# A fused attention, gated-MLP and normalised-MLP kernel on one core: first-block subtractions, weight loads, and places of tiles in SBUF

## The chip, the cores and the metric

One core of a Trainium2 chip (trn2) runs the whole kernel in one launch. The metric is device time in microseconds (us) of that core, median of several runs; lower is better. Engines are called as in the profile: PE (TensorE matmuls), PEld (TensorE weight loads), DVE (VectorE), ACT (ScalarE), POOL (GpSimd), SP (SyncE, which issues all DMAs here). TensorE's clock has two levels, 1.2 and 2.4 GHz; the profile shows which was granted.

## What is computed

Three stages, each fed by the one before; all in float32.

```python
# attention, chunked: 8 batches x 8 heads x 9 chunks of 64 positions, head size 64
attn = softmax(q_c @ k_c.T / 8);  x = attn @ v_c            # -> 4608 tokens x 512
# gated MLP, 512 -> 2048 -> 512
h = x @ w_in;  g = h * clip(h + 3, 0, 6) / 6;  x = g @ w_out
# second MLP, 512 -> 1024 -> 512
h = x @ w_in2; s = h * softmax(h); ln = (s - mean(s)) / sqrt(var(s) + 1e-6) * g_ln
out = ln @ w_out2
```

## The kernel before

**Split products.** Each large matrix product is made of three matmuls in the type float32r: every operand is held as a high part (a rounding cast on ACT, `split`, L73) and a low part (source minus high part, a subtraction on DVE or POOL, L74), and hi x hi, lo x hi and hi x lo are added up in PSUM. One such matmul is 128x128 (stationary, a weight load of its own each time) by 128x512 (moving). There are 5184 of them: 9 blocks x 16 slices x 24 in the gated MLP and 36 tiles x 48 in the second MLP.

**Weights.** The weights arrive as 64-bit words that hold doubles (`fetch`, L127). Each 128x512 slice is turned into a float32 pair in steps: `rescale` (L139, ACT, one operation), `convert` (L144, DVE: one `bitwise_and` for the sign, L152, and two shift-and-or operations, L157), then `split_w` (L170: the cast on ACT, the subtraction on POOL). `wi` are slices of w_in, `wo` of w_out.

**Order.** The program is in a hand-written order; each engine takes its own instructions strictly in the order in which the code issues them. First comes a start section (L322 to L377): four attention units (128 tokens each, scores, softmax, transposition, product with v) that make block 0's input. Then the gated MLP runs over 9 blocks of 512 tokens (L428 to L458). A block has 16 slices f: `moe_h` (L267, 12 matmuls into `hp`, then a Relu on ACT), `moe_g` (L281: the gate on DVE, L282, then the split of g into `g_hi`, `g_lo`), and, one slice later, `moe_o` (L292, 12 matmuls into four `acc` tiles). `slot` puts the attention work of the next block between them, one unit per four slices. In block 0 the weights are still being converted: each slice also issues `convert(("o", f), ("i", f + 3))`, and the subtractions for `g_lo`, `wo` and `wi` are on POOL. The result of a block goes to DRAM (`x2d`). In the second MLP a tile of 128 tokens takes 24 matmuls in `h2` (L474, stationary x, moving `wi`) and 24 in `out_t` (L557, stationary `l_hi` and `l_lo`, moving `wi`), with the softmax and normalisation on ACT, DVE and POOL between them.

**Loads at the start.** SP issues in order: q and k of four units, v, and among them w_in slices 0, 1, w_out slice 0, w_in 2, w_out 1, the norm weights; then q and k of unit 4, v of units 4 and 5, q and k of unit 5 (L367), and only then the remaining weights (L368 to L374).

**Places in SBUF.** The pools are laid out one after the other, and each tile is rounded up to 32 bytes per partition. The first large tile starts at byte 17088 of a partition (16384 reserved, four constants of 32, `ident` 512, `three` 32, `g_sb` 32), which is 64 past a multiple of 128; everything large behind it has a size that is a multiple of 2048, so x, `wi`, `wo`, `g_hi` and `g_lo` all start 64 bytes past a multiple of 128. In the second MLP, pool `b2` has small tiles (128x1 numbers, 32 bytes each, two buffers) between the large ones; behind them `l_hi` and `l_lo` (pool `b3`) come to stand exactly on a multiple of 128 (173056 and on). All offsets inside these tiles that a matmul uses are multiples of 512 bytes.

Of the kernel before, what the change touches and what calls it, by code (L numbers as in the profile page):

```python
# [8 lines left out]
F32 = mybir.dt.float32  # L9
F32R = mybir.dt.float32r  # L10
# [6 lines left out]
P = 128  # L17
# [4 lines left out]
def tile_kernel(  # L22
# [120 lines left out]

    def convert(*keys):  # L144

        work = []
# [4 lines left out]
        for key, r, s in work:  # L151
            nc.vector.tensor_single_scalar(  # L152
                out=s, in_=r[:, :, 1], scalar=-(1 << 31), op=ALU.bitwise_and
            )
        for w, op, shift in ((0, ALU.logical_shift_right, 29), (1, ALU.logical_shift_left, 3)):
            for key, r, s in work:
                nc.vector.scalar_tensor_tensor(  # L157
                    out=s, in0=r[:, :, w], scalar=shift, in1=s, op0=op, op1=ALU.bitwise_or
                )
        for (kind, f), r, s in work:  # L160
            w = s.bitcast(F32)
            if kind == "2" and f >= KD * NS:
                nc.vector.tensor_scalar_mul(
                    out=w, in0=w, scalar1=g_sb[:, f - KD * NS : f - KD * NS + 1]
                )
            t = SLOTS[kind](f, F32R)
# [41 lines left out]

    def attn_exp_act(u):
        sc, mx = exps.pop(u)  # L210
        p_t[u] = att_tile(ap2, "p")
        sums[u] = ap2.tile([P, H], F32, tag="sm", name="sm")
        for h in range(H):
# [41 lines left out]

    def attn_pv(u, pb, x_hi, x_lo, ps=att_psum):
# [8 lines left out]
        split(x_hi[:, :, o : o + P], x_lo[:, :, o : o + P], xps)  # L265

# [13 lines left out]

    def moe_g(hp, t, eng):  # L281
        nc.vector.scalar_tensor_tensor(  # L282
            out=t, in0=t, scalar=6.0, in1=hp, op0=ALU.min, op1=ALU.mult
        )
        g_hi = gp.tile([P, BT], F32R, tag="g_hi", name="g_hi")
        g_lo = gp.tile([P, BT], F32R, tag="g_lo", name="g_lo")
        split(g_hi, g_lo, t, eng)
        return g_hi, g_lo
# [31 lines left out]
    vs = wo_slot(NF - 7, F32).rearrange("p c (h k) -> p c h k", h=H)  # L320

    load_qk(0)  # L322
    load_qk(1, qps[0][:, 0], diagonal(kbs[1], nc.gpsimd))
    load_qk(2, qps[1][:, 0], diagonal(kbs[2], nc.vector))
    fetch("i", 0)
    load_qk(3, qps[2][:, 0], diagonal(kbs[3], nc.gpsimd))
    load_v(0)
    load_v(1)
    fetch("i", 1)
    load_v(2, vs[:, 0])  # L330
    load_v(3, vs[:, 1])
    fetch("o", 0)
    fetch("i", 2)
    fetch("o", 1)
    nc.sync.dma_start(out=g_sb, in_=g_ln)
    make_identity(nc, ident)
    diagonal(pbd, nc.gpsimd)
    nc.gpsimd.memset(three, 3.0)
    xs = new_x()
    attn_scores(0)  # L340
    attn_scores(1)
    load_qk(4)
    attn_norm(0, nc.gpsimd)
# [3 lines left out]
    attn_norm(1)
    attn_scores(3, h_psum, qps[1][:, 1])
    attn_transpose(1, kbs[1])
    attn_norm(2)  # L350
    attn_pv(0, pbd, *xs)
# [14 lines left out]
    attn_scores_act(4)
    load_qk(5)  # L367
    for f in range(2, NF):  # L368
        if f < NF - 7:
            fetch("o", f)  # L370
        if f + 1 < NF:
            fetch("i", f + 1)
    for f in range(NF - 7, NF):
        fetch("o", f)  # L374
    convert(("i", 2))
    rescale("o", 0)
    rescale("i", 3)  # L377
# [25 lines left out]
    def slot(b, f):  # L403
        ph = (f + 1) % 4
        u = (b + 1) * UPB + (f + 1) // 4
        if ph == 0:
            w = u - 1
            if w < NU:
                attn_pv(w, pbd, *xn[w // UPB])
                p_t.pop(w, None)  # L410
                load_v(w + 2)
            start_scores(u)
        elif u < NU:
            first = u < 2 * UPB
            if ph == 1:
                if u in exps:
                    attn_exp_act(u)
                attn_norm(u)
            elif ph == 2 and not first:
                attn_transpose_dve(u, (0, 1))  # L420
# [53 lines left out]
    def h2(t):  # L474
# [19 lines left out]
        mu = b2.tile([P, 1], F32, tag="mu", name="mu")  # L494
        nc.vector.scalar_tensor_tensor(
# [150 lines left out]
```

## Time and profile before

| | us |
|---|---|
| median of 3 runs | 1312.58 (1311.85 to 1313.03) |
| the profiled execution | 1311.98 |
| its span in the trace | 1310.0 |
| start section, to the first `hp` matmul of block 0 | 27.81 |
| block 0, from there to the first matmul of block 1 | 119.02 |
| block 1 (blocks 2 to 6 are as long) | 95.93 |
| PE busy | 1277.4 (98%) |
| DVE, ACT, POOL busy | 794.0, 581.8, 298.5 |

How to read it: the profiled execution lies 0.6 us under the median, and 2 us of it lie outside the span. A "busy" PE counts a matmul from its start to its end; since successive matmuls overlap, that says little on how fast they follow each other. For this the starts of a group and of the next one are used: the difference, divided by the number of matmuls, is called the spacing here.

### The profile page before, as it was taken

What the parts mean: (1) busy time and instruction counts of PE and PEld (TensorE: products, weight loads), DVE (VectorE), ACT (ScalarE), POOL (GpSimd) and SP (SyncE); (2) the same over time, 40 slices, a digit from 0 to 9 for tenths busy, and PEclk for the clock granted to TensorE, in tenths of its full rate; (3) what the DMA queues carried; (4) which work ended last, traced back from release to release, by engine and by line L of the source; (5) the groups of instructions that cost most, each with busy time, mean ns of one, the idle gap of its engine ahead of it and who ended that gap; (6) DMA issues with size and microseconds to landing.
All of it is one profiled execution on the core that took longest, in us unless ns stands there. A gap on an engine that the chain in (4) does not pass through costs nothing.

```text
span 1310.0 us, 17877 instructions
## 1 busy us (share of the span) xinstructions
PE 1277.4 (98%) x6368; PEld 1041.7 (80%) x6368; DVE 794.0 (61%) x1556; ACT 581.8 (44%) x1106; POOL 298.5 (23%) x562
## 2 busy tenths in 40 slices
PE   6699999999999999999999999999999999999998
PEld 5566788888888888888888888888888888888887
DVE  6788655655655655656555555469766555555542
ACT  4566422222322222222322222445687666666665
POOL 2465200000000000000000000355355444444444
PEclk9899999999999999999999999999999999999999
DMA  7910110110110210200200200444132221222111
GB/s 236 409 62 25 57 49 25 57 49 25 58 47 25 77 29 25 81 25 25 81 25 28 78 25 1 129 129 129 28 94 82 80 81 49 81 81 73 57 49 57
DMA packets 52649, 92.41 MB, mean 71 GB/s; under 512 B 9552, under 2 KB 18768, under 8 KB 52560
## 3 DMA queue, kind: packets, MB, share of 16 engines
q1 hardware_dynamic: 52560, 91.27, 21.8%
q8 instruction: 50, 0.82, 0.2%
q14 instruction: 39, 0.32, 0.1%
HBM read 62.92 MB, written 18.87 MB: 62 GB/s over the span
## 4 chain that ended last, share of the span: by engine, by line
PE 89%; issue 3%; POOL 3%; DVE 2%; DMA 1%; ACT 1%; SPq 1%; POOLq 0%; ACTq 0%; DVEq 0%
PE acc L298 27%; PE hp L272 26%; PE po L564 15%; PE hp L482 15%; PE att L261 2%; PE att L186 2%; POOL g_lo L74 1%; POOL wo L74 1%; DMA wi<-in_moe_w_in 1%; DVE s L157 1%; POOL wi L74 1%; DVE s L152 1%; SPq L112 0%; DVE x_lo L74 0%; DVE t L282 0%
## 5 line engine op out<-in xcount | busy, mean ns | idle before, releaser
L298 PE MATMUL acc<-g_hi,wo 128*128 128x512 f32 x1152 | 295.0, 397 | 16.1 <-ACT wo L73 14.2
L272 PE MATMUL hp<-x_hi,wi 128*128 128x512 f32 x1152 | 285.1, 390 | 0.0
L298 PEld LDWEIGHTS acc<-g_hi,wo 128*128 128x128 f32 x1152 | 213.1, 189 | 73.1 <-ACT wo L73 18.9
L278 ACT ACTIVATE t<-hp,three 128x512 f32<-128x512 f32 x144 | 99.0, 687 | 372.6 <-PE hp L272 372.2
L272 PEld LDWEIGHTS hp<-x_hi,wi 128*128 128x128 f32 x1152 | 215.9, 188 | 44.9 <-ACT wi L142 0.2
L282 DVE SCALAR_TENSOR_TENSOR t<-t,hp 128x512 f32<-128x512 f32 x144 | 99.1, 688 | 234.4 <-ACT t L278 234.4
L74 POOL TENSOR_TENSOR g_lo<-t,g_hi 128x512 fp32r<-128x512 f32 x32 | 45.8, 1431 | 715.1 <-PE acc L298 672.5
L482 PE MATMUL hp<-wi,x_hi 128*128 128x512 f32 x576 | 177.8, 390 | 0.0
L298 PE MATMUL acc<-g_lo,wo 128*128 128x512 f32 x576 | 154.4, 390 | 0.0
L272 PE MATMUL hp<-x_lo,wi 128*128 128x512 f32 x576 | 153.9, 389 | 0.0
L564 PE MATMUL po<-wi,l_hi 128*128 128x512 f32 x576 | 140.2, 396 | 0.0
L251 DVE STREAM_TRANSPOSE pbd<-p 32x128 f32<-32x128 f32 x448 | 135.3, 302 | 5.7
L73 ACT CAST g_hi<-t 128x512 fp32r<-128x512 f32 x144 | 89.3, 620 | 107.9 <-DVE t L282 107.9
L564 PEld LDWEIGHTS po<-wi,l_hi 128*128 128x128 f32 x576 | 108.3, 188 | 25.6
L482 PEld LDWEIGHTS hp<-wi,x_hi 128*128 128x128 f32 x576 | 108.2, 188 | 23.5
L298 PEld LDWEIGHTS acc<-g_lo,wo 128*128 128x128 f32 x576 | 108.6, 189 | 22.9
L74 POOL TENSOR_TENSOR l_lo<-m,l_hi 128x1024 fp32r<-128x1024 f32 x36 | 86.6, 2406 | 174.1 <-ACT l_hi L73 152.0
L272 PEld LDWEIGHTS hp<-x_lo,wi 128*128 128x128 f32 x576 | 108.1, 188 | 22.5
L74 DVE TENSOR_TENSOR g_lo<-t,g_hi 128x512 fp32r<-128x512 f32 x112 | 77.6, 693 | 76.8 <-ACT g_hi L73 76.8
L516 ACT COPY m<-tr 32x256 f32<-32x256 f32 x288 | 115.8, 402 | 2.9
L482 PE MATMUL hp<-wi,x_lo 128*128 128x512 f32 x288 | 112.4, 390 | 0.0
L491 ACT ACTIVATE e<-hp,nmx 128x1024 f32<-128x1024 f32 x36 | 40.2, 1116 | 111.3 <-DVE nmx L488 111.3
(91 smaller groups left out, 1299.7 us busy)
## 6 DMA issues: line engine op xcount, KB each, us to landing
wi<-in_moe_w_in SPq DMA_DIRECT2D x24, 512.0 KB, 7.3
x2d<-xo SPq DMA_DIRECT2D x36, 256.0 KB, 2.8
xo<-x2d SPq DMA_DIRECT2D x36, 256.0 KB, 4.3
m<-tr SPq DMA_DIRECT2D x288, 32.0 KB, 1.8
out<-ob SPq DMA_DIRECT2D x36, 256.0 KB, 2.2
v<-in_v SPq DMA_DIRECT2D x34, 256.0 KB, 2.6
q<-in_q SPq DMA_DIRECT2D x33, 256.0 KB, 3.5
kbd<-in_k SPq DMA_DIRECT2D x66, 128.0 KB, 3.5
```

Source lines behind the costliest of these rows:

```text
L73: nc.scalar.copy(out=hi, in_=src)
L74: (eng or nc.vector).tensor_sub(out=lo, in0=src, in1=hi.bitcast(F32))
L186: nc.tensor.matmul(sc[r0 : r0 + D, h // 2], qt[:, h], kt[:, :, h], start=True, stop=True)
L251: nc.vector.transpose(out=pb[o : o + 32, s // 2, c, s % 2], in_=pv[s * 32 : s * 32 + 32, c, e],)
L272: nc.tensor.matmul(hp, wi[f][:, a, kk * P : (kk + 1) * P], b[:, kk], start=(n == 0), stop=(n == 3 * KD - 1),)
L278: nc.scalar.activation(out=t, in_=hp, func=AF.Relu, bias=three[:])
L282: nc.vector.scalar_tensor_tensor(out=t, in0=t, scalar=6.0, in1=hp, op0=ALU.min, op1=ALU.mult)
L298: nc.tensor.matmul(acc[dc], wo[f][:, w, dc * P : (dc + 1) * P], g[i], start=(f == 0 and n == 0), stop=(f == NF - 1 and n == 2),)
L482: nc.tensor.matmul(hp[:, s * DM : (s + 1) * DM], a[:, kk, o : o + P], wi[kk * NS + s][:, w], start=(n == 0), stop=(n == 3 * KD - 1),)
L491: nc.scalar.activation(out=e, in_=hp, func=AF.Exp, bias=nmx, accum_out=r)
L516: move(out=m[b * 32 : b * 32 + 32, a], in_=tr[a * 32 : a * 32 + 32, b])
L564: nc.tensor.matmul(po, a[:, f], wi[KD * NS + f][:, w], start=(n == 0), stop=(n == 3 * NF2 - 1),)
```

## The change

1. **Subtractions.** In block 0 the subtractions for `g_lo`, `wo` and `wi` move from POOL to DVE; one softmax normalisation of the start (unit 2) moves from DVE to POOL. Conversion and split are cut into smaller functions so that they can be interleaved: in each slice of block 0 DVE now takes the gate, a first weight subtraction, the next signs, `g_lo`, the other weight subtractions, and then the shift-and-or operations. A w_out slice is converted one slice earlier than before. In the start section the scores go to the idle `acc` PSUM tiles and the first products with v to `hp` tiles.
2. **Weights queued first.** Two weight loads follow the loads of unit 4's q and k, others follow v of units 4 and 5; q and k of unit 5 and the norm weights come later.
3. **Projection operands at equal places.** The small tiles of the second MLP get a pool of their own (`bs`) behind the large ones, and `l_hi`, `l_lo` become six named single tiles. With that (and 4.) they stand at the same place modulo 2048 as x, `wi`, `wo`, `g_hi` and `g_lo`.
4. **64 bytes.** `three` is allocated with 17 columns instead of 1 (68 bytes, rounded to 96), so every large tile behind it moves by 64: the first starts at 17152, a multiple of 128, and so do all the others, `l_hi` and `l_lo` included.

The number and shapes of the matmuls are unchanged. The core of the diff:

```diff
-    three = const.tile([P, 1], F32, name="three")
+    three = const.tile([P, 17], F32, name="three")[:, :1]
...
+    def split_w_hi(n=1):
+        while ready and n:
+            hi, lo, w = ready.pop(0)
+            nc.scalar.copy(out=hi, in_=w)
+            halves.append((hi, lo, w))
+            n -= 1
+
+    def split_w_lo(eng):
+        for hi, lo, w in halves:
+            eng.tensor_sub(out=lo, in0=w, in1=hi.bitcast(F32))
+        halves.clear()
...
-    attn_scores(2, h_psum, qps[0][:, 1])
-    attn_transpose(0, pbd, h_psum)
-    rescale("i", 0)
+    attn_scores(2, acc_psum(2), qps[0][:, 1])
+    attn_transpose(0, pbd)
...
+    split_w(1, nc.vector)
     rescale("i", 1)
-    attn_transpose(3, kbs[3], h_psum)
-    split_w(1)
-    attn_pv(2, kbs[2], *xs)
+    attn_pv(2, kbs[2], *xs, h_psum, lo=False)
+    rescale("o", 0)
...
     pend = []
+    ahead = [[("o", f + 1), ("i", f + 3)] for f in range(NF)]
+    ahead[0].insert(0, ("i", 2))
...
-            h = moe_h(f, *xn[b])
+            hp, t = moe_h(f, *xn[b])
+            moe_gate(hp, t)
             if first:
-                split_w(1)
-            pend.append((b, f, moe_g(*h, nc.gpsimd if first or last else nc.vector)))
+                split_w(1, nc.vector)
+                g = moe_split(t, nc.vector, lambda: convert_signs(*ahead[f]))
+                split_w_hi(4)
+                split_w_lo(nc.vector)
+                convert_words()
+            else:
+                g = moe_split(t, nc.gpsimd if last else nc.vector)
+            pend.append((b, f, g))
             if f % 4 == 3:
                 slot(b, f)
-            if first:
-                convert(("o", f), ("i", f + 3))
...
-    b3 = ctx.enter_context(tc.tile_pool(name="b3", bufs=3, reuse_waits="tile"))
+    b3 = ctx.enter_context(tc.tile_pool(name="b3", bufs=1, reuse_waits="tile"))
+    bs = ctx.enter_context(tc.tile_pool(name="bs", bufs=2, reuse_waits="tile"))
...
-        l_hi = b3.tile([P, NF2, P], F32R, tag="l_hi", name="l_hi")
-        l_lo = b3.tile([P, NF2, P], F32R, tag="l_lo", name="l_lo")
+        l_hi, l_lo = l_tile("l_hi", t % 3), l_tile("l_lo", t % 3)
```

How it moves instructions, at the three places that the prediction speaks of. First SP, the DMA queue, from the first weights on. Before:

```order
L135 DMA wo_133<-in_moe_w_out 128x1024
L135 DMA wi_135<-in_moe_w_in 128x1024
L135 DMA wo_137<-in_moe_w_out 128x1024
L335 DMA g_sb<-in_moe_g_ln 128x8
L110 DMA q<-in_q 128x512
L112 DMA kbd<-in_k 64x512 x2
L120 DMA v<-in_v 128x512 x2
L110 DMA q<-in_q 128x512
L112 DMA kbd<-in_k 64x512 x2
L135 DMA wo_336<-in_moe_w_out 128x1024
L135 DMA wi_338<-in_moe_w_in 128x1024
```

Now:

```order
L135 DMA wo_133<-in_moe_w_out 128x1024
L135 DMA wi_135<-in_moe_w_in 128x1024
L110 DMA q<-in_q 128x512
L112 DMA kbd<-in_k 64x512 x2
L135 DMA wo_178<-in_moe_w_out 128x1024
L135 DMA wi_180<-in_moe_w_in 128x1024
L120 DMA v<-in_v 128x512
L135 DMA wo_250<-in_moe_w_out 128x1024
L135 DMA wi_252<-in_moe_w_in 128x1024
L120 DMA v<-in_v 128x512
L135 DMA wo_283<-in_moe_w_out 128x1024
L135 DMA wi_285<-in_moe_w_in 128x1024
```

The fourth w_in slice (`wi_338` before, `wi_180` now) moved from behind the second q and k pair to right behind the first.

Second, DVE from the scores of unit 4 (`mx<-att`) to the gate of slice 0 (`t<-t,hp`). Before:

```order
L205 TENSOR_REDUCE mx<-att 128x8
L206 TENSOR_SCALAR mx<-mx 128x8
L152 TENSOR_SCALAR s<-wi_135 128x512
L157 SCALAR_TENSOR_TENSOR s<-wi_135,s 128x512 x2
L282 SCALAR_TENSOR_TENSOR t<-t,hp 128x512
```

Now, to the first `g_lo`:

```order
L223 TENSOR_REDUCE mx<-att 128x8
L224 TENSOR_SCALAR mx<-mx 128x8
L151 TENSOR_SCALAR s<-wi_131 128x512
L159 SCALAR_TENSOR_TENSOR s<-wi_131,s 128x512 x2
L151 TENSOR_SCALAR s<-wo_133 128x512
L186 TENSOR_TENSOR wi_387<-s,wi_387 128x512
L159 SCALAR_TENSOR_TENSOR s<-wo_133,s 128x512 x2
L311 SCALAR_TENSOR_TENSOR t<-t,hp 128x512
L186 TENSOR_TENSOR wo_394<-s,wo_394 128x512
L151 TENSOR_SCALAR s<-wi_135 128x512
L151 TENSOR_SCALAR s<-wo_178 128x512
L321 TENSOR_TENSOR g_lo<-t,g_hi 128x512
```

The second w_in slice and the first w_out slice are now converted between the scores and the first gate, and three subtractions stand on DVE.

Third, one later slice of block 0 on DVE. Before:

```order
L282 SCALAR_TENSOR_TENSOR t<-t,hp 128x512
L152 TENSOR_SCALAR s<-wo_336 128x512
L152 TENSOR_SCALAR s<-wi_346 128x512
L157 SCALAR_TENSOR_TENSOR s<-wo_336,s 128x512
L157 SCALAR_TENSOR_TENSOR s<-wi_346,s 128x512
```

Now:

```order
L311 SCALAR_TENSOR_TENSOR t<-t,hp 128x512
L186 TENSOR_TENSOR wo_479<-s,wo_479 128x512
L151 TENSOR_SCALAR s<-wo_283 128x512
L151 TENSOR_SCALAR s<-wi_285 128x512
L321 TENSOR_TENSOR g_lo<-t,g_hi 128x512
L186 TENSOR_TENSOR wi_480<-s,wi_480 128x512
L159 SCALAR_TENSOR_TENSOR s<-wo_283,s 128x512
L159 SCALAR_TENSOR_TENSOR s<-wi_285,s 128x512
```

In both, two more shift-and-or operations follow. A slice has seven DVE operations before and ten now; POOL has three subtractions per slice before and none now. The weights subtracted now (`wo_479`, `wi_480`) were shifted one slice earlier.

## Rows read from the trace of the kernel before

**Rows 1.** The page: busy times; the chain that ended last, by engine.

```profile
PE 1277.4 (98%) x6368; PEld 1041.7 (80%) x6368; DVE 794.0 (61%) x1556; ACT 581.8 (44%) x1106; POOL 298.5 (23%) x562
PE 89%; issue 3%; POOL 3%; DVE 2%; DMA 1%; ACT 1%; SPq 1%; POOLq 0%; ACTq 0%; DVEq 0%
```

**Rows 2.** Busy time by stretch: window, length, engines with counts, clock, DMA.

```profile
27.81:47.98 20.17, 10.59 (x39) 8.31 (x38) 15.34 (x21) 10.56 (x30) 8.52 (x6) 0.75 0.92 354
47.98:146.83 98.85, 92.35 (x482) 69.67 (x481) 80.10 (x113) 59.31 (x137) 53.93 (x40) 1.00 0.30 108
146.83:242.76 95.93, 95.93 (x514) 79.07 (x513) 57.04 (x127) 28.75 (x58) 1.29 (x1) 1.00 0.15 45
935.00:1283.50 348.50, 348.50 (x1513) 284.06 (x1512) 198.07 (x389) 243.33 (x486) 163.34 (x424) 1.00 0.23 70
```

**Rows 3.** The chain in order of time, second MLP: start, length, what.

```profile
907.82 21.76 PE hp L482 x96
...
1195.18 5.60 PE po L564 x24
1200.78 5.47 PE hp L482 x24
...
1283.71 22.41 PE po L564 x96
```

**Rows 4.** PE's timeline in block 6: start, length, matmuls; one slice from start to start.

```profile
703.95 1.98 PE L272 MATMUL hp<-x_hi,wi 128*128 128x512 f32 x8
...
709.39 0.39 PE L272 MATMUL hp<-x_hi,wi 128*128 128x512 f32 x1
```

**Rows 5.** PE's timeline: matmuls at 1.2 GHz; transpositions at 2.4 GHz, four and one.

```profile
43.12 3.78 PE L298 MATMUL acc<-g_hi,wo 128*128 128x512 f32 x8 [9.58 <-ACT wo L73]
...
43.71 2.77 PE L298 MATMUL acc<-g_hi,wo 128*128 128x512 f32 x6
...
46.70 1.43 PE L298 MATMUL acc<-g_lo,wo 128*128 128x512 f32 x4
...
138.81 0.60 PE L236 MATMUL att<-ident,p 128*128 128x128 f32 x4
...
138.81 0.27 PE L236 MATMUL att<-ident,p 128*128 128x128 f32 x1
```

**Rows 6.** PE's timeline where `h2` follows `out_t`.

```profile
1200.61 0.62 PE L482 MATMUL hp<-wi,x_hi 128*128 128x512 f32 x2
...
1202.00 0.62 PE L482 MATMUL hp<-wi,x_hi 128*128 128x512 f32 x2
```

**Rows 7.** Timeline of the first slices of block 0.

```profile
35.80 0.65 ACT L142 ACTIVATE wi<-wi 128x512 f32<-128x512 f32 x1 [5.99 <-DMA wi<-in_moe_w_in]
36.35 0.67 ACT L278 ACTIVATE t<-hp,three 128x512 f32<-128x512 f32 x1
...
43.12 0.80 PE L298 MATMUL acc<-g_hi,wo 128*128 128x512 f32 x1 [9.58 <-ACT wo L73]
```

**Rows 8.** Timeline in block 0: DVE alone, then DVE beside POOL.

```profile
62.10 0.42 DVE L152 TENSOR_SCALAR s<-wi 128x512 int32<-128x512 int32 x1
62.44 0.69 DVE L157 SCALAR_TENSOR_TENSOR s<-wo,s 128x512 int32<-128x512 int32 x1
63.04 0.69 DVE L157 SCALAR_TENSOR_TENSOR s<-wi,s 128x512 int32<-128x512 int32 x1
...
66.36 1.29 POOL L74 TENSOR_TENSOR wi<-s,wi 128x512 fp32r<-128x512 f32 x1
66.40 1.54 DVE L152 TENSOR_SCALAR s<-wo 128x512 int32<-128x512 int32 x1
```

**Rows 9.** Groups of instructions: count, busy, mean ns of one, idle before.

```profile
L282 DVE SCALAR_TENSOR_TENSOR t<-t,hp 128x512 f32<-128x512 f32 x144 | 99.1, 688 | 234.4 <-ACT t L278 234.4
L74 DVE TENSOR_TENSOR g_lo<-t,g_hi 128x512 fp32r<-128x512 f32 x112 | 77.6, 693 | 76.8 <-ACT g_hi L73 76.8
L228 DVE TENSOR_TENSOR p<-p,sm 128x512 f32<-128x512 f32 x33 | 26.8, 811 | 1.1
```

More of the change, by code (lines that the diff above doesn't have):

```diff
@@ L142, in rescale, with convert_signs @@
             nc.scalar.activation(out=r, in_=r, func=AF.Copy, scale=2.0**-112)
-    def convert(*keys):
-        work = []
+    work, ready, halves = [], [], []
+    def convert_signs(*keys):
         for key in keys:
@@ L150, in convert, with convert_words @@
                 work.append((key, raws.pop(key).bitcast(I32), s))
[L151 to L154, printed above, removed]
+                nc.vector.tensor_single_scalar(
+                    out=s, in_=work[-1][1][:, :, 1], scalar=-(1 << 31), op=ALU.bitwise_and
+                )
+    def convert_words():
         for w, op, shift in ((0, ALU.logical_shift_right, 29), (1, ALU.logical_shift_left, 3)):
@@ L168, in convert, with split_w @@
             ready.append((t[:, 0], t[:, 1], w))
-    def split_w(n=2):
+        work.clear()
+    def convert(*keys):
+        convert_signs(*keys)
+        convert_words()
+    def split_w_hi(n=1):
         while ready and n:
-            split(*ready.pop(0), nc.gpsimd)
+            hi, lo, w = ready.pop(0)
+            nc.scalar.copy(out=hi, in_=w)
+            halves.append((hi, lo, w))
             n -= 1
+    def split_w_lo(eng):
+        for hi, lo, w in halves:
+            eng.tensor_sub(out=lo, in0=w, in1=hi.bitcast(F32))
+        halves.clear()
+    def split_w(n=2, eng=None):
+        split_w_hi(n)
+        split_w_lo(eng or nc.gpsimd)
     def att_psum():
@@ L207, in attn_scores_act, with attn_exp_act @@
         exps[u] = sc, mx
[L209 to L213, printed above, removed]
+    def attn_exp_act(u, heads):
+        sc, mx = exps[u]
+        if u not in sums:
+            p_t[u] = att_tile(ap2, "p")
+            sums[u] = ap2.tile([P, H], F32, tag="sm", name="sm")
+        for h in heads:
             nc.scalar.activation(
@@ L254, in attn_transpose_dve, with attn_pv @@
                     )
-    def attn_pv(u, pb, x_hi, x_lo, ps=att_psum):
+    def attn_pv(u, pb, x_hi, x_lo, ps=att_psum, lo=True):
         vt = v_t.pop(u)
@@ L264, in attn_pv, with attn_lo @@
         o = (u % UPB) * P
-        split(x_hi[:, :, o : o + P], x_lo[:, :, o : o + P], xps)
+        hi, lo_ = x_hi[:, :, o : o + P], x_lo[:, :, o : o + P]
+        nc.scalar.copy(out=hi, in_=xps)
+        los.append((lo_, xps, hi))
+        if lo:
+            attn_lo()
+    los = []
+    def attn_lo():
+        lo, xps, hi = los.pop(0)
+        nc.vector.tensor_sub(out=lo, in0=xps, in1=hi.bitcast(F32))
     def moe_h(f, x_hi, x_lo):
@@ L279, in moe_h, with moe_gate @@
         return hp, t
-    def moe_g(hp, t, eng):
+    def moe_gate(hp, t):
         nc.vector.scalar_tensor_tensor(
@@ L284, in moe_g, with moe_split @@
         )
+    def moe_split(t, eng, between=None):
         g_hi = gp.tile([P, BT], F32R, tag="g_hi", name="g_hi")
         g_lo = gp.tile([P, BT], F32R, tag="g_lo", name="g_lo")
-        split(g_hi, g_lo, t, eng)
+        nc.scalar.copy(out=g_hi, in_=t)
+        if between:
+            between()
+        eng.tensor_sub(out=g_lo, in0=t, in1=g_hi.bitcast(F32))
         return g_hi, g_lo
@@ L320, in tile_kernel, with acc_psum, later @@
     vs = wo_slot(NF - 7, F32).rearrange("p c (h k) -> p c h k", h=H)
+    def acc_psum(i):
+        return lambda: ps_acc.tile([P, DM], F32, tag=f"acc{i}", name=f"acc{i}")
+    def later(f):
+        if f < NF:
+            fetch("i", f)
     load_qk(0)
@@ L328, in tile_kernel @@
     load_v(1)
-    fetch("i", 1)
+    fetch("i", 0)
     load_v(2, vs[:, 0])
     load_v(3, vs[:, 1])
+    fetch("i", 1)
     fetch("o", 0)
     fetch("i", 2)
-    fetch("o", 1)
-    nc.sync.dma_start(out=g_sb, in_=g_ln)
     make_identity(nc, ident)
@@ L339, in tile_kernel @@
     xs = new_x()
-    attn_scores(0)
-    attn_scores(1)
+    attn_scores(0, acc_psum(0))
+    attn_scores(1, acc_psum(1))
     load_qk(4)
+    fetch("o", 1)
+    fetch("i", 3)
     attn_norm(0, nc.gpsimd)
-    attn_scores(2, h_psum, qps[0][:, 1])
-    attn_transpose(0, pbd, h_psum)
-    rescale("i", 0)
[L347 to L351, printed above, removed]
+    attn_scores(2, acc_psum(2), qps[0][:, 1])
+    attn_transpose(0, pbd)
+    attn_norm(1)
+    attn_scores(3, acc_psum(3), qps[1][:, 1])
+    attn_transpose(1, kbs[1])
+    rescale("i", 0)
+    attn_norm(2, nc.gpsimd)
+    attn_pv(0, pbd, *xs, h_psum, lo=False)
     load_v(4)
-    attn_transpose(2, kbs[2], h_psum)
+    fetch("o", 2)
+    fetch("i", 4)
+    convert(("i", 0))
+    attn_transpose(2, kbs[2])
     attn_norm(3)
-    convert(("i", 0))
-    attn_pv(1, kbs[1], *xs)
+    attn_pv(1, kbs[1], *xs, h_psum, lo=False)
     load_v(5)
-    rescale("i", 1)
-    attn_transpose(3, kbs[3], h_psum)
-    split_w(1)
-    attn_pv(2, kbs[2], *xs)
+    fetch("o", 3)
+    fetch("i", 5)
+    fetch("o", 4)
+    fetch("i", 6)
+    attn_lo()
+    attn_transpose(3, kbs[3])
+    attn_lo()
+    split_w(1, nc.vector)
+    rescale("i", 1)
+    attn_pv(2, kbs[2], *xs, h_psum, lo=False)
+    rescale("o", 0)
+    attn_lo()
+    attn_pv(3, kbs[3], *xs, h_psum, lo=False)
+    attn_lo()
+    attn_scores_act(4)
+    for f in range(5, NF):
+        if f == 6:
+            load_qk(5)
+            nc.sync.dma_start(out=g_sb, in_=g_ln)
+        fetch("o", f)
+        later(f + 2)
     convert(("i", 1))
-    attn_pv(3, kbs[3], *xs)
+    split_w_hi()
+    convert_signs(("o", 0))
+    split_w_lo(nc.vector)
+    convert_words()
     rescale("i", 2)
-    split_w(1)
[L366 to L376, printed above, removed]
+    rescale("o", 1)
     rescale("i", 3)
@@ L416, in slot @@
                 if u in exps:
[L417 to L420, printed above, removed]
+                    attn_exp_act(u, range(H // 2))
+                else:
+                    attn_norm(u)
+            elif ph == 2:
+                if u in exps:
+                    attn_exp_act(u, range(H // 2, H))
+                    attn_norm(u)
+                if not first:
+                    attn_transpose_dve(u, (0, 1))
             elif ph == 3:
@@ L445, in tile_kernel @@
             if first:
-                rescale("o", f + 1)
+                rescale("o", f + 2)
                 rescale("i", f + 4)
-            split_w(1 if first else 2)
+            else:
+                split_w(2)
             if last:
@@ L546, in chain_rstd, with l_tile @@
         rs_t[t] = y
+    def l_tile(name, i):
+        return b3.tile([P, NF2, P], F32R, tag=f"{name}{i}", name=f"{name}{i}")
     def split_l(t):
```

21 lines of the change are left out of this document (11 added, 10 removed).

## The prediction

> **What bounds the kernel now.** I read the page first: PE is busy for 98% of the span, and the chain that ended last is 89% PE [rows 1]. So time can come from two places only: stretches in which PE waits, and the spacing of PE's own matmuls.
>
> The stretches: from slice 2 of block 0 to block 1, PE is busy 92.35 of 98.85 us; before that, from 27.81 to 47.98, it is busy for about half, and the granted clock is 0.75 [rows 2]. Block 1, with the same matmuls, takes 95.93 us, block 0 119.02: 23 us at the start are not the matmuls'.
>
> The spacing: in the gated MLP one slice of 24 matmuls goes from 703.95 to 709.39, 226.7 ns each [rows 4]. In the second MLP, the 96 matmuls of four `h2` in a row take 21.76 us, again 226.7 ns; the 96 of four `out_t` in a row take 22.41 us, 233.4 ns; alternating, it is 5.60 us per 24 (233.3) in `out_t` and 5.47 (227.9) in `h2` [rows 3]. After an `out_t` the first six of `h2` are slow, 1.39 us or 232 ns each, and the rest run at 226.7 [rows 6]. Shapes and types are the same everywhere, the moving operand of `out_t` is `wi` as in `h2`; only the place of the stationary operand differs (a multiple of 128 against 64 past one). **So places in SBUF cost time here**; that is what parts 3 and 4 of the change touch.
>
> How much of 226.7 is more than the matmul itself? 512 columns at 2.4 GHz are 213.3 ns. At 1.2 GHz the same matmuls (seven between 43.71 and 46.70) stand 427 ns apart, which is 512 columns at 1.2 GHz with nothing on top [rows 5]. So the 13.3 ns on top at 2.4 GHz are no fixed work of each matmul that can't be hidden; they show when operands have to be delivered at twice the rate. And 13.3 ns are 32 columns, in float32 128 bytes: 226.67 is 17/16 of 213.33. A moving row of 2048 bytes that begins 64 past a multiple of 128 touches 17 pieces of 128 bytes, one that begins on a multiple touches 16. That fits to the tenth of a ns, but no row shows a moving operand at another place, so it stays an inference.
>
> **The change, part by part.**
>
> *Subtractions and early weights, up to slice 2.* Before, ACT stood 5.99 us before a `rescale`, because the fourth w_in slice came late, and the Relu of slice 0 stood behind it until 36.35; PE then idled 9.58 us, to 43.12, and afterwards ran at 1.2 GHz, 427 ns instead of 227 for some ten matmuls, 2 us [rows 5, 7]. Now this load stands right behind unit 4's q and k, so I take the wait as gone. What is late next is DVE. I take the first `hp` matmul at about 27 (27.81 before; DVE sheds a normalisation and one slice's conversion ahead of it, and takes on one subtraction). From the last `x_lo`, 0.7 us later, DVE has in its order: maximum and scaling, 1.0; sign and two shift-and-or operations for `wi`, 1.6; sign, 0.4; subtraction, 0.7; two shift-and-or for `wo`, 1.2; gate, 0.7; subtraction, 0.7; three signs, 1.0; `g_lo`, 0.7; four more shift-and-or, 2.4. That is 10.4 us at 0.60 to 0.69 per operation [rows 8, 9], with a cast on ACT and hand-overs some 11.4, so slice 2 starts at about 39, not at 47.98: **9 us less** (bounds: 4, if a load or a cast holds it up, to 11).
>
> *The rest of block 0.* Before: 98.85 us for 14 slices, 7.06 each [rows 2]. POOL's three subtractions per slice also held DVE up: a sign takes 0.42 us alone and 1.54 beside POOL [rows 8]. Now POOL is silent. DVE per slice: gate 0.69, two signs 0.7, four shift-and-or at 0.60, three subtractions at 0.69 [rows 8, 9], 5.9 us, and per four slices one unit's attention (x_lo 0.7, maximum 1.0, normalisation 1.2), 0.7 per slice: 6.6 at most. PE per slice: 24 matmuls, 5.44, attention as in block 1 0.56, transpositions 0.15 (0.60 per four slices [rows 5]): 6.15. I take 6.35 and 14 x 0.71 = **10 us less** (bounds from 6.6 and 6.15 per slice: 6 to 13). The added waits of DVE for ACT's casts are covered by the next signs, which stand between; if that cover is missing, the slice goes towards 6.6 and over. Together 19 us less, bounds 10 to 24. Moving a normalisation to POOL, the PSUM tiles used at the start, and the later norm weights (first used in the last block) cost nothing that PE waits for.
>
> *Equal places alone.* 864 matmuls of `out_t` from 233.3 to 226.7: 5.8 us; the slow six after each of 36 `out_t`, 0.03 us each time: 1.1 us.
>
> *64 bytes.* If the 17/16 is the reason, all spacing at 2.4 GHz falls to 213.3 and whatever then shows. Transpositions, whose identity does stand on a multiple of 128, follow each other by (0.60 - 0.27) / 3 = 0.110 us [rows 5]; that is 128 columns at two periods each, 106.7, and some 3 ns. So I take 216. Outside block 0, where DVE sets the pace, there are 8 x 384 + 864 = 3936 matmuls at 226.7: 3936 x 10.7 = 42 us; and 864 at 233.3: 864 x 17.3 = 15 us. The bounds: 213.3 below (52 and 17 us), no gain above. I take the low value since it rests on a ratio that fits exactly, and on the fact, shown, that 64 bytes matter.
>
> The Trainium skill (TensorE: Matmul & The Clock Gate, "Wait — 56ns, not 53.3ns?") gives columns / 2.4 plus about 2.5 ns, measured as 215.7 for 512 columns in bf16. The trace before disagrees by 11 ns for these float32r matmuls; by that figure the two terms would be 43 and 15 us, the sum 1234.
>
> **Sum**, against the profiled execution (1311.98; the median is 0.6 more): 1312 - 19 - 42 - 15 - 1 = **1235 us**. In block 1 DVE is busy 57 of 96 us and in the second MLP ACT 243 of 348 [rows 2]; with PE 5% faster both still have room, so neither becomes the bound.
>
> **The rivals.**
>
> *Only the relation of the two operands counts*, not the distance from a multiple of 128. For: the slow `out_t` differs from `h2` in just that relation, and the slow six show a state that comes and goes between weight load and matmul. Against: it gives no reason for exactly 32 columns in a settled stream. The move by 64 bytes then does nothing: 1312 - 19 - 5.8 - 1.1 = 1286. Chance 0.27.
>
> *The multiple of 128 is itself the slow place.* `l_hi` and `l_lo` are the only float32r operands that stand there before, and theirs are the slowest matmuls. Then all others come down to them: 3936 x 6.7 = 26 us more, `out_t` as before: 1312 - 19 + 26 = 1319, slower. It decides as soon as the spacing in the gated MLP rises by more than 19 us / 3936 = 5 ns. Against: a place that is bad for a weight load need not be bad for the moving operand, which is what fills the time, and the 17/16 points the other way. Chance 0.07.
>
> *Half of it.* The moving stream gets faster, but then collides with the weight loads beside it, which so far it does not: spacing 221, 3936 x 5.4 + 864 x 12 = 32 us: 1312 - 19 - 32 - 1 = 1260. Chance 0.08.
>
> *Places change nothing*, and `out_t` is slow for a reason of its own, its 24 matmuls into one PSUM bank instead of two. 1312 - 19 = 1293. Chance 0.06. The Trainium skill (SBUF — State Buffer, "Door 1", the note on cachelines) speaks for this rival: lines are 16 bytes, and both places are multiples of 16, so by it neither part 3 nor part 4 should be seen. Rows 3 speak against that, as far as the stationary operand goes.
>
> **How the numbers follow.** The forecast has what is left, 0.52: 1235, by its own bounds 1223 to 1250. For 8 in 10 the range must reach over the half case and the relation case, to 1286 and a start section that gives little: 1223 to 1292. A measurement of this kernel tells some 0.2% from no change, 2.6 us. All cases but the second rival are faster: 0.91; 0.02 for a start section that loses what the places give; slower 0.07.
>
> **What would show it.** Right: an `hp` slice of 24 matmuls from start to start in 5.2 us; four `out_t` in a row at the same spacing; slice 2 of block 0 near 39 us and block 1 near 128; no stretch of the clock at 1.2 GHz after slice 0; signs on DVE near 0.42 throughout block 0. Wrong: a slice at 5.44 again (then 1286), or at 5.60 (then 1319); DVE waiting for ACT's casts between subtractions, with more than 7 us per slice; a wait for a weight load in slices 0 to 3.

## The result, and the profile after

| | before | after |
|---|---|---|
| median, us | 1312.80 (1311.85 to 1313.52, 4 runs) | 1288.74 (1288.35 to 1290.17, 4 runs) |
| ratio of the times, 95% interval | | 0.9819 (0.9802 to 0.9836) |
| span of the profiled execution, us | 1310.0 | 1286.9 |

The change makes the kernel 24 us faster. The forecast was 1235 us, a gain of 77, with a range of 1223 to 1292. The sign is right and the time lies in the range, near its slow end; the size is wrong by 54 us, and the time is that of the first rival, "only the relation of the two operands counts" (1286).

The page of after, busy times and the chain that ended last by engine (against [rows 1]):

```profile
PE 1265.0 (98%) x6368; PEld 1041.7 (81%) x6368; DVE 793.8 (62%) x1603; ACT 580.9 (45%) x1106; POOL 234.5 (18%) x515
PE 94%; DVE 3%; ACT 1%; issue 1%; DMA 0%; SPq 0%; ACTq 0%; DVEq 0%
```

PE is 94% of the chain instead of 89%. POOL's 3% have left it, and POOL was busy 64 us less.

Busy time by stretch, after (window, length, then each engine's busy time with counts, clock, DMA share, GB/s): slices 0 and 1, the rest of block 0, block 1, the second MLP. They answer to [rows 2].

```profile
27.78:40.11 12.33, 9.15 (x36) 6.52 (x36) 11.54 (x22) 7.53 (x19) 0.00 (x0) 1.00 1.03 393
40.11:129.28 89.17, 88.66 (x481) 72.38 (x482) 85.78 (x162) 62.51 (x149) 0.00 (x0) 0.98 0.33 125
129.28:226.08 96.80, 96.29 (x514) 79.16 (x513) 56.00 (x125) 28.14 (x57) 0.00 (x0) 1.00 0.15 44
...
890.88:1286.90 396.02, 391.83 (x1729) 324.13 (x1727) 225.64 (x439) 271.31 (x542) 183.60 (x472) 1.00 0.23 72
```

Slice 2 of block 0 starts at 40.11 (before 47.98), block 1 at 129.28 (146.83): 17.6 us have gone there. For the rest of block 0 PE waits only twice, ahead of slice 2's first matmul (to 40.11) and within slice 2 (to 41.81):

```profile
PE hp L301 <- ACT wi L180: 1.6, 1, 1.6
PE hp L301 <- DVE wi L186: 0.5, 1, 0.5
```

From 41.81 to block 1 the chain of work that ended last is PE alone. Where no attention work stands between them, slices follow each other by 5.44 us, as in the later blocks:

```profile
56.15 1.98 PE L301 MATMUL hp<-x_hi,wi 128*128 128x512 f32 x8
...
61.59 1.98 PE L301 MATMUL hp<-x_hi,wi 128*128 128x512 f32 x8
```

Four slices with their attention take 24.37 us (48.46 to 72.83, and again to 97.20), 6.09 each. So from there on PE sets the pace; DVE, busy 85.78 of 89.17 us, only just keeps up. Block 1 got 0.87 us longer (95.93 before); 0.5 of that is one wait of `att` for DVE's transpositions.

The chain in the second MLP of after (start, length, what), against [rows 3]:

```profile
891.03 21.76 PE hp L549 x96
912.79 5.44 PE po L633 x24
...
1260.95 21.77 PE po L633 x96
```

`out_t` now takes 5.44 us per 24 matmuls, 226.7 ns each, as `h2` does (21.76 per 96); before it was 5.60, and 5.47 in the `h2` behind it. Its 24 matmuls still go into one PSUM bank, so the bank was not the reason. From the first `h2` to the end of the last `out_t` it is 1282.72 - 891.03 = 391.69 us instead of 1306.12 - 907.82 = 398.30: 6.6 us less. But nothing went below 226.7. PE's timeline in the gated MLP of after, one slice from start to start, where [rows 4] had 5.44 us:

```profile
687.17 1.98 PE L301 MATMUL hp<-x_hi,wi 128*128 128x512 f32 x8
...
692.61 1.98 PE L301 MATMUL hp<-x_hi,wi 128*128 128x512 f32 x8
```

It is 5.44 still. So the gain is 17.6 - 0.9 + 6.6 = 23.3 us, and of the 42 and 15 us forecast for the move by 64 bytes only the 5.8 of equal places are there. The experiments had to settle why, and which parts carry what there is.

**Theory A**: for PE's operands only their relation to each other counts; the 13.3 ns above 512 columns at 2.4 GHz have another cause. **Theory B**: the place itself counts too.

### The profile page after: what moved, and what is told of

Same layout as the page of the kernel before. It is cut to its first block, busy times and chain, and to the rows that moved or that the text cites. A ratio compares the mean times of both kernels' runs of the same rounds, so it can differ in the third digit from the quotient of the medians.

```text
span 1286.9 us, 17808 instructions
## 1 busy us (share of the span) xinstructions
PE 1265.0 (98%) x6368; PEld 1041.7 (81%) x6368; DVE 793.8 (62%) x1603; ACT 580.9 (45%) x1106; POOL 234.5 (18%) x515
## 4 chain that ended last, share of the span: by engine, by line
PE 94%; DVE 3%; ACT 1%; issue 1%; DMA 0%; SPq 0%; ACTq 0%; DVEq 0%
PE acc L332 30%; PE hp L301 29%; PE po L633 15%; PE hp L549 15%; PE att L280 3%; PE att L204 2%; DVE s L159 1%; DVE t L311 0%; DVE pbd L270 0%; DMA wo<-in_k 0%; DVE s L151 0%; DVE x_lo L74 0%; ACT wi L142 0%; PE att L255 0%; PE acc L204 0%
## 5 line engine op out<-in xcount | busy, mean ns | idle before, releaser
L332 PE MATMUL acc<-g_hi,wo 128*128 128x512 f32 x1152 | 289.5, 393 | 0.6 <-ACT g_hi L318 0.6
L301 PEld LDWEIGHTS hp<-x_hi,wi 128*128 128x128 f32 x1152 | 215.7, 188 | 50.1 <-ACT wi L180 3.4
L321 POOL TENSOR_TENSOR g_lo<-t,g_hi 128x512 fp32r<-128x512 f32 x16 | 23.3, 1457 | 827.1 <-ACT g_hi L318 827.1
L318 ACT CAST g_hi<-t 128x512 fp32r<-128x512 f32 x144 | 89.3, 620 | 109.0 <-DVE t L311 109.0
L633 PE MATMUL po<-wi,l_hi 128*128 128x512 f32 x576 | 136.4, 389 | 0.0
L321 DVE TENSOR_TENSOR g_lo<-t,g_hi 128x512 fp32r<-128x512 f32 x128 | 88.5, 692 | 76.9 <-ACT g_hi L318 76.8
```

The lines of the kernel that those rows point to most:

```text
L301: nc.tensor.matmul(hp, wi[f][:, a, kk * P : (kk + 1) * P], b[:, kk], start=(n == 0), stop=(n == 3 * KD - 1),)
L318: nc.scalar.copy(out=g_hi, in_=t)
L321: eng.tensor_sub(out=g_lo, in0=t, in1=g_hi.bitcast(F32))
L332: nc.tensor.matmul(acc[dc], wo[f][:, w, dc * P : (dc + 1) * P], g[i], start=(f == 0 and n == 0), stop=(f == NF - 1 and n == 2),)
L633: nc.tensor.matmul(po, a[:, f], wi[KD * NS + f][:, w], start=(n == 0), stop=(n == 3 * NF2 - 1),)
```

## The experiments

**1 and 2. The 64 bytes alone, both ways.** Taken out of the changed kernel (`e1_after_no_shift`), and put into the kernel before (`e2_before_shift`):

```diff
-    three = const.tile([P, 17], F32, name="three")[:, :1]
+    three = const.tile([P, 1], F32, name="three")
```

> The changed kernel with the constant back at one column, so that every large tile, l_hi and l_lo included, stands 64 past a multiple of 128 again; all else as changed. Theory A, only the relation between the two operands counts: 1289 us (within 2), 24 matmuls of the gated MLP in 5.44 us, of the projection in 5.44. Theory B, the multiple of 128 itself is worth something that another loss hides: over 1292, with a longer spacing somewhere.

> The kernel before with only the constant at 17 columns: x and the weights come to a multiple of 128, the projection's operands move with them to 64 past one. Theory A (relation): no difference, 1312.5 (within 2), the projection still at 233 ns. Theory B (the place itself): the projection's or the gated MLP's spacing moves by more than 1 ns, the time by over 3 us.

Measured: without the shift 1288.69 us (1288.31 to 1290.10), beside 1288.74 with it. Before with the shift: 1311.78 beside 1312.06, ratio 0.9999 (0.9990 to 1.0009). The chain of the kernel before with the shift:

```profile
1007.06 5.60 PE po L564 x24
```

`out_t` keeps its 5.60 although its weights now stand on a multiple of 128 and `l_hi` does not: which of the two stands where is indifferent. That also rules out the rival by which the multiple of 128 is itself the slow place. Part 4 is worth nothing, to within 0.1%.

**3. Block 0's subtractions back on POOL**, the rest of the change kept:

```diff
-                split_w(1, nc.vector)
-                g = moe_split(t, nc.vector, lambda: convert_signs(*ahead[f]))
+                split_w(1, nc.gpsimd)
+                g = moe_split(t, nc.gpsimd, lambda: convert_signs(*ahead[f]))
...
-                split_w_lo(nc.vector)
+                split_w_lo(nc.gpsimd)
```

> The changed kernel with block 0's subtractions of the weights and of g_lo on GpSimd again, the order and the loads as changed. If the subtractions' engine gives most of block 0's gain: 1296 to 1300, slices of block 0 near 7 us, the sign operations on VectorE at 0.9 to 1.5 us. If the gain is from converting one slice earlier: within 2 us of 1289, slices still near 6.2.

Measured: 1306.30 us (1304.78 to 1307.70), 17.6 more than the change, and more than the 1296 to 1300 that was expected. It is as much as the whole change gains in block 0. The stretch from slice 2 to block 1 in this run:

```profile
42.37:146.56 104.19, 92.56 (x480) 74.36 (x481) 101.33 (x118) 62.16 (x149) 64.12 (x44) 0.95 0.26 97
```

It takes 104.19 us against 89.17, with 44 operations on POOL, and DVE is busy for longer (101.33) although it has 44 operations fewer: here DVE sets the pace. DVE's groups of instructions in that stretch show why (count, busy, mean ns of one, idle before), first in this run:

```profile
L159 DVE SCALAR_TENSOR_TENSOR s<-wo,s 128x512 int32<-128x512 int32 x28 | 35.2, 1257 | 0.1
L159 DVE SCALAR_TENSOR_TENSOR s<-wi,s 128x512 int32<-128x512 int32 x25 | 24.6, 985 | 0.0
L151 DVE TENSOR_SCALAR s<-wo 128x512 int32<-128x512 int32 x14 | 12.3, 880 | 0.0
L151 DVE TENSOR_SCALAR s<-wi 128x512 int32<-128x512 int32 x12 | 11.6, 968 | 0.0
L311 DVE SCALAR_TENSOR_TENSOR t<-t,hp 128x512 f32<-128x512 f32 x15 | 10.2, 677 | 0.6 <-ACT t L307 0.5
L247 DVE TENSOR_TENSOR p<-p,sm 128x512 f32<-128x512 f32 x4 | 5.6, 1402 | 0.1
...
L223 DVE TENSOR_REDUCE mx<-att 128x8 f32<-128x512 f32 x4 | 2.7, 676 | 0.0
```

and then in the change itself:

```profile
L159 DVE SCALAR_TENSOR_TENSOR s<-wo,s 128x512 int32<-128x512 int32 x28 | 19.2, 686 | 0.1
L159 DVE SCALAR_TENSOR_TENSOR s<-wi,s 128x512 int32<-128x512 int32 x25 | 17.1, 686 | 0.0
...
L311 DVE SCALAR_TENSOR_TENSOR t<-t,hp 128x512 f32<-128x512 f32 x15 | 10.2, 681 | 2.4 <-ACT t L307 2.4
...
L151 DVE TENSOR_SCALAR s<-wo 128x512 int32<-128x512 int32 x14 | 5.9, 421 | 0.0
L151 DVE TENSOR_SCALAR s<-wi 128x512 int32<-128x512 int32 x12 | 5.1, 422 | 0.0
L247 DVE TENSOR_TENSOR p<-p,sm 128x512 f32<-128x512 f32 x4 | 2.8, 692 | 0.1
```

Beside POOL a shift-and-or takes 1257 or 985 ns instead of 686, a sign 880 or 968 instead of 421, the normalisation 1402 instead of 692. Operations that take a large input from PSUM (the gate from `hp`, 677; the maximum from `att`, 676) are not touched. The four groups of shift-and-or and sign and the normalisation are 39 us longer than in the change (89.3 against 50.1), 0.89 us for each of the 44 subtractions on POOL; on DVE one takes 0.69. In the view of waits, PE stands 11.2 us for the normalisation, in four waits. The 104.19 us are also 5.3 more than in the kernel before (98.85), which has its subtractions on POOL too: without their move to DVE the new order is a loss there. Which part of the new order that is was not tried, nor was the move in the old order.

The Trainium skill (SBUF — State Buffer, "SBUF: two separate sides") says that VectorE and GpSimd share a pair of ports as an exclusive lock, which a VectorE operation needs when it runs in a two-port mode or, beside a GpSimd operation that reads SBUF, has two SBUF inputs. The rows agree: what stretches has its large inputs in SBUF, and the gate, with one of its two in PSUM, stays at 677.

**4. The loads back in the old order**, the rest kept:

```diff
     load_qk(2, qps[1][:, 0], diagonal(kbs[2], nc.vector))
+    fetch("i", 0)
...
     load_qk(4)
-    fetch("o", 1)
-    fetch("i", 3)
...
     load_v(4)
-    fetch("o", 2)
-    fetch("i", 4)
...
```

> The changed kernel with the loads in the order of before (unit 5's q and k ahead of the fourth slice of w_in). If the early loads give the gain up to slice 2: 1296 to 1299, a wait of ScalarE for a weight load of some 5 us and a stretch at 1.2 GHz after slice 0. If the order on VectorE gives it: within 2 us of 1289.

Measured: 1292.02 us (1290.82 to 1293.13), 3.3 more, between the two outcomes that were expected. The wait of [rows 7] is back, but shorter, and PE's wait with it:

```profile
37.43 0.65 ACT L142 ACTIVATE wi<-wi 128x512 f32<-128x512 f32 x1 [2.65 <-DMA wi<-in_moe_w_in]
...
40.08 2.61 PE L332 MATMUL acc<-g_hi,wo 128*128 128x512 f32 x8 [3.37 <-ACT g_hi L318]
```

ACT stands 2.65 us before the rescaling instead of 5.99, and PE idles 3.37 us instead of 9.58. The early loads are thus worth some 3 us beside the new order on DVE. The traces of runs 3 and 4 show where the two parts count:

| us | before | run 3 | run 4 | the change |
|---|---|---|---|---|
| first `hp` to slice 2 | 20.17 | 13.32 | 15.07 | 12.33 |
| slice 2 to block 1 | 98.85 | 104.19 | 88.93 | 89.17 |

The loads matter ahead of slice 2 (2.7 us), the subtractions mostly behind it (1.0 and 15.0). Some 4 of the 7.8 us gained ahead of slice 2 come back in neither run: the order on DVE may carry them, or either part alone, which is not shown. Nothing is read here from when the first `hp` comes: in the change and in runs 1 and 5 to 10, whose start is the same code, that lies anywhere between 27.62 and 29.76.

**5 and 6. The distance between the operands.** In the changed kernel the `l` tiles are moved by a few bytes against the weights, another distance for each of three tiles in turn:

```diff
-        return b3.tile([P, NF2, P], F32R, tag=f"{name}{i}", name=f"{name}{i}")
+        k = (32, 64, 96)[i] // 4
+        wide = b3.tile([P, NF2 * P + DM], F32R, tag=f"{name}{i}", name=f"{name}{i}")
+        return wide[:, k : k + NF2 * P].rearrange("p (f j) -> p f j", j=P)
```

(16, 128, 256 in the second run; each was run once, and only the spacing is read from it. Apart from tiles that are 2048 bytes larger, only the distance differs from the change.)

> The changed kernel with the projection's stationary operand moved against its moving one by 32, 64 and 96 bytes (tiles t with t mod 3 = 0, 1, 2). Theory A (relation, period 128): 64 gives 233 ns again, 32 and 96 something between 227 and 240, none under 226.7 if 226.7 is the bare matmul; if the 13.3 ns on top of 512 columns are a collision of the two streams, some offset gives 214 to 222.

> As the run before with 16, 128 and 256 bytes. Theory A with a period of 128 bytes: 128 and 256 give 226.7 like 0; with a longer period they differ from it. 16 tells whether the step is finer than 32.

The chain of the first run, three tiles in turn, then of the second:

```profile
1002.11 5.61 PE po L635 x24
...
1013.19 5.59 PE po L635 x24
...
1024.23 5.60 PE po L635 x24
```

```profile
1012.46 5.44 PE po L635 x24
...
1023.35 5.59 PE po L635 x24
...
1034.39 5.44 PE po L635 x24
```

All of 32, 64 and 96 cost: 5.59 to 5.61 us per 24 matmuls. Of 16, 128 and 256 only one costs, and by the tiles' turn it is 128; 16 and 256 run at 5.44. One step of 64 bytes is no special case: every distance tried from 32 to 128 costs 6 to 7 ns per matmul, 16 and 256 none.

**7 and 8. What are the 13.3 ns?** Other sizes in `out_t`, then other types and data, again three tiles in turn, each run once and read for the spacing only:

```diff
...
-                        po, a[:, f], wi[KD * NS + f][:, w],
+                            po[:m, c0:c1], a[:, f, :m], wi[KD * NS + f][:, w, c0:c1],
...
```

```diff
...
+                    if t % 3 == 0:
+                        mv = wb[:, f]
+                    elif t % 3 == 1:
+                        mv = mv[:, None, :P].to_broadcast([P, 4, P])
...
```

> The changed kernel; the projection of tiles t mod 3 = 0 in two halves of 256 columns, of 1 in pieces of 384 and 128, of 2 with 64 of 128 stationary columns (half of the rows left out, the other half written twice). If the 13.3 ns are fixed per matmul: 256 columns 120 ns, 384 columns 173. If they are a share of the columns (17/16): 113 and 170. If they are the weight load beside the stream, one period for each 16 bytes of it: 64 stationary columns give 220.

> The changed kernel; the projection of tiles t mod 3 = 0 from bf16 copies of both operands (high parts only, so less exact), of 1 with a moving operand that repeats its first 128 columns four times (products left out), of 2 unchanged. If the 13.3 ns come from delivering 4 bytes per column: bf16 214 to 217 ns. If they belong to each matmul whatever its type: bf16 226.7. Repeating 512 bytes four times: 226.7 if the rate counts, less if fetching new bytes counts.

PE's timeline of the first run: two halves of 256 columns, then 384 and 128. Behind it the chain of the same run, at the tile with 64 stationary columns and at that of 384 and 128:

```profile
1052.63 2.08 PE L638 MATMUL po<-wi,l_hi 128*128 128x256 f32 x16
...
1055.51 2.08 PE L638 MATMUL po<-wi,l_hi 128*128 128x256 f32 x16
...
1063.85 2.96 PE L638 MATMUL po<-wi,l_hi 128*128 128x384 f32 x16
...
1068.04 1.90 PE L638 MATMUL po<-wi,l_hi 128*128 128x128 f32 x16
```

```profile
1041.83 5.52 PE po L638 x24
...
1064.02 6.81 PE po L638 x48
```

From start to start, 24 matmuls of 256 columns take 2.88 us, 120.0 ns each; 24 of 384 take 4.19, 174.6. At 2.4 GHz the columns alone are 106.7 and 160.0: on top stand 13.3 and 14.6, as with 512 columns. A share of 1/16 would be 6.7 and 10. So it is a **fixed 13 to 15 ns per matmul**. Halving the stationary operand's columns doesn't lower it (5.52 per 24, 230 ns).

The chain of the second run: a tile of bf16 operands (24 matmuls from 1011.50 to 1016.70), then a float32r tile whose moving operand repeats its first 128 columns:

```profile
1011.50 0.23 PE po L644
1011.73 0.05 issue
1011.79 4.91 PE po L644 x22
1016.70 5.46 PE hp L550 x24
1022.16 5.44 PE po L644 x24
```

bf16: 5.20 us per 24, 216.7 ns. Repeated columns: 5.44, no gain. So 10 of the 13.3 ns go with the type, and none with the number of fresh bytes. Both operands were bf16 in that tile; which of the two matters was not tried.

The Trainium skill (TensorE: Matmul & The Clock Gate, "Wait — 56ns, not 53.3ns?") gives a fixed cost per matmul that shows at 2.4 GHz and not at 1.2, 215.7 ns for 512 columns. The bf16 tile agrees with 216.7; float32r has the same kind of cost, but 10 ns more of it than the bf16 tile.

**9. Equal places alone**, part 3 undone in the changed kernel (`l_hi`, `l_lo` and the small tiles as before):

```diff
-    b3 = ctx.enter_context(tc.tile_pool(name="b3", bufs=1, reuse_waits="tile"))
-    bs = ctx.enter_context(tc.tile_pool(name="bs", bufs=2, reuse_waits="tile"))
+    b3 = ctx.enter_context(tc.tile_pool(name="b3", bufs=3, reuse_waits="tile"))
...
-        l_hi, l_lo = l_tile("l_hi", t % 3), l_tile("l_lo", t % 3)
+        l_hi = b3.tile([P, NF2, P], F32R, tag="l_hi", name="l_hi")
+        l_lo = b3.tile([P, NF2, P], F32R, tag="l_lo", name="l_lo")
...
```

> Part 3 undone in the changed kernel: small tiles of the second MLP back between the l tiles, so that l_hi and l_lo stand 64 bytes (modulo 256) from the second MLP's weights again. A (the relation of the two operands): out_t matmuls at 233.3 ns instead of 226.7, the first six of each h2 after an out_t at 232: 864 x 6.6 + 36 x 0.03 = 6.8 us more than the change, 1295.5; the start as in the change (block 1 at 129.3). B (only the place itself, or chance): 1288.7, nothing. By the traces A: 1295.5, bounds 1294 to 1297.

Measured: 1294.99 us (1294.89 to 1295.23), 6.3 more than the change and as expected, with `out_t` at 5.60 and the `h2` behind it at 5.47:

```profile
1001.19 5.60 PE po L630 x24
1006.79 5.47 PE hp L548 x24
```

Here the weights stand on a multiple of 128 and `l` is 64 off; before it was the other way round, with the same times. Theory A holds, and part 3 carries the whole gain of the second MLP.

**10. A version that uses it.** Two of three matmuls multiply a low part, which needs few bits. From tile 8 of the second MLP on those two are made in bf16; `high by high` stays float32r:

```diff
+            ] if t < 8 else [
+                (a[:, kk, o : o + P], w[kk * NS + s])
+                for a, w in ((x_hi, whi), (x_lo[:, 1], wlb), (x_lo[:, 0], whb)) for kk in range(KD)
+            ]
...
+                nc.gpsimd.tensor_copy(out=d[f], in_=wi[f][:, i].bitcast(F32))
```

> The change, and from tile 8 of the second MLP on the two products that hold a low part are made of bf16 operands (the low part, and a bf16 copy of the other operand's high part; low parts are rounded to bf16); high by high stays float32r. Added: 32 copies of weights on GpSimd in tiles 0 to 7, four casts per x block and one of 1024 columns per tile on ScalarE. If the 13.3 ns are fixed work of a float32r matmul and nothing else changes, 28 tiles x 32 bf16 matmuls at 216 instead of 226.7: 896 x 10.7 = 9.6 us less than the change, 1279.1. Rival 1: each passage from float32r to bf16 and back costs (a weight load that can't lie beside the other type's matmul, 64 to 128 columns, 27 to 53 ns): 28 tiles x 3 groups x 2 passages x 27 to 53 ns = 4.5 to 9 us given back, 1283.6 to 1288. Rival 2: ScalarE, at 243 of 348 us busy, with some 1.5 us more per tile (of 10.9) becomes late and PE waits for l: slower than 1288.7. Most likely 1280, bounds 1278 to 1290.

Measured: 1283.75 us (1283.12 to 1284.40), ratio to before 0.9787 (0.9772 to 0.9801): 5.0 us below the change, or 4.2 by the two ratios to before; 9.6 were expected. The chain behind the switch, then PE's timeline in one `h2` and the start of the next group:

```profile
1006.38 5.34 PE hp L562 x24
1011.73 5.32 PE po L660 x24
```

```profile
1006.03 1.28 PE L562 MATMUL hp<-wi,x_hi 128*128 128x512 f32 x4
1007.15 1.90 PE L562 MATMUL hp<-wb,x_lo 128*128 128x512 bf16 x8
1008.70 1.28 PE L562 MATMUL hp<-wi,x_hi 128*128 128x512 f32 x4
```

A tile of 48 matmuls takes 5.34 + 5.32 = 10.66 us instead of 10.88. With 16 matmuls at 226.7 ns and 32 at run 8's 216.7 it would be 10.56. So 0.10 us per tile, some 35 ns for each of its three groups of bf16, is given back, which is rival 1, below its price (28 x 0.10 = 2.8 us in all, where it had 4.5 to 9). The recorded starts don't show on which side of a group it is lost: from 1006.03 four float32r matmuls take 1.12 us (0.91 at 226.7), but the eight in bf16 behind them 1.55, which is less than their columns alone (8 x 213.3 ns). Only the sum of both, 2.67, can be used.

The second MLP gives 28 x 0.22 = 6.2 us, less 0.6 for which PE waits near the end; traced it is 386.03 us (892.66 to 1278.69) instead of 391.69. In this profile 1.6 us of it don't arrive, since the second MLP starts at 892.66 and in the change at 891.03. Of that 1.4 is there at the first `hp` (29.20 against 27.78), the spread of the start named under run 4. ScalarE, rival 2, has room: PE waits for nothing else in the second MLP.

## Why the prediction was right or wrong

**Wrong: "64 bytes. If the 17/16 is the reason, all spacing at 2.4 GHz falls to 213.3".** This is the step that failed: 57 us of the 77 rested on it, and only the 5.8 of equal places came. It had three supports. The first: at 1.2 GHz matmuls stand 427 ns apart with nothing on top [rows 5], so the 13.3 ns "are no fixed work of each matmul that can't be hidden". Run 7 shows that they are fixed, 13 to 15 ns at 256, 384 and 512 columns; that a cost doesn't show at the lower clock does not make it a matter of bytes. The second: 226.67 is 17/16 of 213.33 to the tenth of a ns. All matmuls of that argument had 512 columns, and with one size a fixed cost of 32 columns and a share of 1/16 are the same number. The fit was no evidence. The third, "the fact, shown, that 64 bytes matter", was shown for the distance between the two operands only (runs 5, 6 and 9). Runs 1 and 2 put the move's worth at zero, and part 4 of the change only looks like part of the gain because it came with parts that have one.

**The rival's weight.** "Only the relation" was given 0.27, held down because it gave "no reason for exactly 32 columns". But the 13.3 ns and the 6.7 ns between [rows 3] and `h2` are two things: one is fixed per matmul and mostly goes with float32r (runs 7 and 8), the other with the distance of the operands (runs 5, 6, 9). A rival need not explain both.

**Right: equal places.** Forecast 5.8 + 1.1 = 6.9 us, traced 6.6, by run 9 6.3.

**Nearly right: up to slice 2.** Forecast 9 us less, measured 47.98 - 40.11 = 7.9. The first `hp` came at 27.78, not at "about 27"; from there to slice 2 it took 12.33 us, where the forecast had 12. The wait for the load is gone, as said, and DVE is what is late next, as said:

```profile
39.44 0.62 ACT L180 CAST wi<-s 128x512 fp32r<-128x512 f32 x1 [1.17 <-DVE s L159]
...
40.11 1.19 PE L301 MATMUL hp<-x_hi,wi 128*128 128x512 f32 x4 [1.64 <-ACT wi L180]
```

How the gain divides is shown only in part: the early loads carry 2.7 of the 7.8 us by run 4, the subtractions 1.0 by run 3.

**Right in size, in part by luck: the rest of block 0.** Forecast 6.35 us per slice, measured 89.17 / 14 = 6.37; 9.7 us less, forecast 10. What held PE up is named rightly: a sign takes 421 ns throughout, as forecast, and run 3 brings the long ones back. But 6.35 was a value taken between DVE's 6.6 and PE's 6.15. The trace shows PE's own pace, 6.09 over four slices, and one slow slice: slice 2 takes 8.35 us (40.11 to 48.46), with a wait and a stretch at 1.2 GHz that the forecast did not have.

**Wrong, small: "no stretch of the clock at 1.2 GHz after slice 0".** There is one. Behind the two waits that end at 40.11 and 41.81 the granted clock is 0.50, which is 1.2 GHz, for 3.42 us:

```profile
42.42:45.84 3.42, 3.42 (x10) 2.64 (x9) 3.42 (x7) 3.38 (x12) 0.00 (x0) 0.50 1.03 414
```

PE is on the chain there: 20 matmuls from 41.81 to 48.10 take 6.29 us, where 226.7 ns each would be 4.53, some 1.8 us less. DVE is busy for all of the 3.42 us too, so how much earlier block 1 would start without this stretch is not shown.

## What to carry to other kernels

A ratio that fits exactly proves nothing where every row has the same size: a cost per instruction and a cost per byte look alike until one size is changed, and here one run with 256 columns would have told them apart. Where PE's stationary and moving operands come from different pools, keep them at the same place modulo 256 bytes, since four of the distances tried cost time; a small tile between large ones can cost 3% of the time of every matmul that reads them (233.3 against 226.7 ns). A subtraction on POOL was not free for DVE: in run 3 it held DVE's SBUF operations up by 0.89 us, more than the 0.69 us that DVE takes to do it.

## What the runs showed of the hardware

- A float32r matmul of 256 to 512 columns at 2.4 GHz takes its columns plus a fixed 13 to 15 ns (226.7 ns at 512, 174.6 at 384, 120.0 at 256); in bf16 512 columns take 216.7. With 128 columns it is 2.62 us per 24 (6.81 - 4.19, the pair's chain against its first half), 109 ns, so that something else sets the pace there.
- A stationary operand that stands 32, 64, 96 or 128 bytes past its moving one (modulo 256) makes a float32r matmul of 512 columns take 233 ns instead of 226.7; 16 and 256 bytes make no difference (runs 5 and 6). Other distances were not tried. Behind a slow `out_t` the first six matmuls of `h2` are slow too [rows 6].
- A group of bf16 matmuls between float32r ones costs some 35 ns in all beside its own spacing (run 10).
- What the 13 ns are, and why they don't show at 1.2 GHz, was not tried.
